# VectorE's operands in a fused attention and feed-forward kernel: q's scale through PSUM, the first keys transposed as fp32

## The chip, the core and the metric

The kernel runs on one NeuronCore of a Trainium2 chip. A core has a matrix engine (TensorE, PE in the profile), a vector engine (VectorE, DVE), an activation engine (ScalarE, ACT), a general engine (GpSimd, POOL) and a synchronisation engine (SyncE, SP) that here issues DMAs. Each works through its own instructions in order; semaphores make one wait for another. On-chip data lie in SBUF, matmul results in PSUM, which has eight banks of 512 fp32 columns for each of 128 partitions. POOL works on data in SBUF alone in this kernel.

The metric is device time in microseconds, the median over several executions of the whole program.

## What is computed

```python
# q, k, v: [8, 8, 576, 64] (batch, head, token, dim); w_phi: [64, 128]
def phi(x):
    proj = np.einsum('bhsd,df->bhsf', x, w_phi)
    proj = proj - np.max(np.abs(proj), axis=-1, keepdims=True)
    return np.concatenate([np.exp(proj), np.exp(-proj)], axis=-1)
q_p, k_p = phi(q), phi(k)
kv  = np.einsum('bhsf,bhsd->bhfd', k_p, v)
z   = np.sum(k_p, axis=2)
num = np.einsum('bhsf,bhfd->bhsd', q_p, kv)
den = np.einsum('bhsf,bhf->bhs', q_p, z)[..., None] + 1e-06
x   = (num / den) -> [4608, 512]
gate = np.maximum(x @ w_gate, 0.0)          # [512, 1536]
out  = (gate * (x @ w_val)) @ w_out         # -> [4608, 512] fp32
```

Linear attention with a feature map, and behind it a gated feed-forward network (FFN). In the feature map each row is shifted by the maximum of its absolute projections. The shift of q cancels between numerator and denominator for exp(proj) and exp(-proj) only up to a factor exp(2 max) between the two halves, so the kernel takes unshifted exponentials and applies that factor later.

## The kernel before

**Tiling.** The 8 batches follow each other. Of each batch's 576 tokens the first 512 are handled as 4 chunks of 128 tokens for each of 8 heads, two heads at a time (u = 0 to 3); the last 64 tokens of all heads are gathered in tiles of their own (names with an m: km, vm, qm). Matmuls run in bf16 with fp32 sums. The FFN runs on groups of 512 tokens: group g is batch g's 512 tokens, a ninth group holds the remaining tokens of all batches. Group 0 is cut into two halves of 256 tokens, so that it can begin after two chunks.

**Steps of a batch.** The keys (kn) are turned so that dim lies on partitions (kT), by PE for batches 0 and 1 (turn_pe), by transposing DMAs on SP's queue afterwards. k_item multiplies two heads with w_phi (L537), takes the row maxima on VectorE (mk, L548) and the exponentials on ScalarE (kp, L511), computes exp(max) and its inverse (ek, L520 and L523) and scales v with them on POOL (vs, L563 and L570). k_rest does the same for the last tokens (kpm, mkm, vsm at L604 and L610); in batch 0 its scaling may go to POOL or VectorE. k_kv multiplies kp with vs (L631) and copies the result to SBUF (kv, L638). For q, q_cols forms the projections (L655), their maxima (mq, L665) and exponentials (qp). q_scale turns the maxima with an fp32 transpose (away, L682), takes a maximum into the SBUF tile xq (L688), spreads it to zq by a product with the constant tile one_a or one_b (L694), and turns it back by a matmul (L702); its exponential is cq. Batch 0 uses q_scale_rows instead (mr at L732, cr at L742). q_num multiplies qp with kv (L763), and VectorE adds the two halves with the scale: t (L771), u (L778), the inverse of the denominator r (L788). The quotient xu (L791) is a product with two SBUF inputs; it is made on POOL, and in batch 0 on POOL or VectorE. xu is transposed to xT, by PE in batch 0 (L804, L811), by DMA on SP later. The FFN takes x to val and gate (L833, L839, L842) and to the output (L864, L874, store L879).

**The start.** The space of w_out (wo_sb) is not needed early, so the first batch's k is loaded as fp32 into wo_sb (in pieces of heads 0-1, 2-3, 4-7 and the last tokens, on SP's queue) and cast to bf16 in kn and km by five casts at L918, on POOL, ScalarE or VectorE; then turned. w_phi's load goes out behind the first piece of k. Other loads: k, v, q of later batches and the weights, on the queues of SP and POOL. POOL issues its loads between its compute instructions, in order. PE fills waits of the first 24 us with matmuls on a tile of zeros (L353).

**Order.** A planner written into the kernel decides it when the program is built: op(...) records each step with the engines that it may run on, a duration for each, what it depends on, the buffers and PSUM banks that it takes, and a key for its priority. Plan.run then plays the steps through and writes each engine's instructions in that order. Changing a duration, an engine or a buffer of one step can change the order of everything after it. FFN steps have a late key and fill what attention leaves free. Loads and DMA transposes are kept apart: transposes wait until the loads issued before them are done, and the other way round.

Of the kernel before, what the change touches and what calls it, by code (L numbers as in the profile page):

```python
# [9 lines left out]
FP32 = mybir.dt.float32  # L10
# [239 lines left out]
def kernel(  # L250
# [11 lines left out]
    nc = tc.nc  # L262
# [23 lines left out]
    def ring(name, n, shape, dtype=BF16):  # L286
# [20 lines left out]
        "mkm": ring("mkm", 2, [P, NU], FP32),  # L307
        "ekm": ring("ekm", 2, [P, NU, 2], FP32),
        "mq": ring("mq", 2, [P, NQ, C * H], FP32),
        "xq": ring("xq", 1, [P, 32], FP32),  # L310
        "zq": ring("zq", 1, [P, NQ, 32], FP32),
        "cq": ring("cq", 2, [P, C * H], FP32),
        "mqm": ring("mqm", 1, [P, NQ, H], FP32),
# [46 lines left out]
    def bank():  # L360
        return Buf(R["ps"])
# [14 lines left out]
            rows_ = slice(D * hh, D * (hh + 1))  # L376
            nc.vector.tensor_copy(w2[rows_, hh, :], w32[rows_])

    o_w32 = op(SP, 0.53, load_w, key=(0, 0.5), kind="l", nbytes=2 * D * F * 4)
    o_w = op(DVE, 0.3, cast_w, [o_w32], key=(2, 0, -30.0))  # L380

    def clear_w():
# [89 lines left out]

    def turn_pe(src, dst, n, dst_buf, deps, key, src_buf):

        ps = bank()

        def mm():
            pt = ps.t.bitcast(BF16)  # L480
            s = src()
            for i in range(n):
                nc.tensor.matmul(
                    pt[:, P * i : P * (i + 1)], lhsT=s[:, P * i : P * (i + 1)], rhs=ident,
                    is_transpose=True,
                )

        def out_(eng):
            f = nc.scalar.copy if eng is nc.scalar else eng.tensor_copy
            f(dst(), ps.t.bitcast(BF16)[:, 0 : n * P])  # L490

        a = op(PE, 0.057 * n, mm, [*deps, o_ident], [src_buf, dst_buf], [ps], key, "a")
        return op((ACT, DVE), {ACT: act(P * n), DVE: 0.06 + 0.0675 * n}, out_, [a], [dst_buf],
                  [ps], key, "a")

    def turn_dma(src, dst, nbytes, dst_buf, deps, key, src_buf, pad=1.0):
        def go():
# [80 lines left out]
    def k_rest(b, kmT, turned, vm, o_v, key, dve_scale=False):  # L578
        kp, m, e, vs = buf("kpm"), buf("mkm"), buf("ekm"), buf("vsm")
        ps = bank()  # L580

        def rows():
            for i in range(2):
                nc.tensor.matmul(
                    ps.t[:, 2 * F * i : 2 * F * (i + 1)],
                    lhsT=kmT.t[:, i, :],
                    rhs=w2.rearrange("p a f -> p (a f)"),
                )

        def amax():  # L590
            nc.vector.tensor_reduce(
                m.t, ps.t.rearrange("p (c f) -> p c f", f=F),
                axis=AX.X, op=ALU.max, apply_absolute_value=True,
            )

        a = op(PE, 0.22, rows, [turned, o_w, o_wz], [kmT, kp, m, e, vs], [ps], key, "a")
        r = op(DVE, 0.6, amax, [a], [m], [ps], key, "a")
        ex = exps(ps, lambda s: kp.t[:, s], kp, [a], key, F)
        o_e = e_of(m, e, [r], key)
        sc = []  # L600
        for x in range(2):
            def scale(eng, x=x):
                rows_ = slice(SM * x, SM * (x + 1))
                eng.tensor_tensor(  # L604
                    vs.t[rows_, :, x, :, 0:D],
                    vm.t[rows_][:, :, None, :].to_broadcast([SM, NU, 2, D]),
                    e.t[rows_][:, :, :, None].to_broadcast([SM, NU, 2, D]),
                    op=ALU.mult,
                )
                eng.tensor_copy(vs.t[rows_, :, x, :, D], e.t[rows_])  # L610

            engs = (POOL, DVE) if dve_scale else (POOL,)
            sc.append(op(engs, {POOL: 1.12, DVE: 1.9}, scale, [o_e, o_v, o_clear], [vm, e, vs],
                         key=key, kind="a"))
        return kp, vs, ex, sc
# [56 lines left out]
            exd.append(exps(ps, dst, qp, [a], key, P))  # L672
        return reds, exd

    def q_scale(mq, xq, zq, cq, n, deps, key):

        ps = bank()
        cols = NQ * n
        one, pick = (one_a, pick_a) if n > H else (one_b, pick_b)

        def away():
            nc.tensor.matmul(  # L682
                ps.t[0:cols, 0:P], lhsT=mq.t.rearrange("p j c -> p (j c)"), rhs=ident32,
                is_transpose=True,
            )

        def amax():
            nc.vector.tensor_reduce(  # L688
                xq.t[0:cols], ps.t[0:cols, 0:P].rearrange("p (g t) -> p t g", g=NQ),
                axis=AX.X, op=ALU.max,  # L690
            )

        def spread():
            nc.vector.tensor_tensor(  # L694
                zq.t[0:cols],
                xq.t[0:cols][:, None, :].to_broadcast([cols, NQ, 32]),
                one[0:cols][:, :, None].to_broadcast([cols, NQ, 32]),
                op=ALU.mult,
            )

        def back():
            nc.tensor.matmul(  # L702
                ps.t[:, P : P + n], lhsT=zq.t[0:cols].rearrange("p j t -> p (j t)"),
                rhs=pick[0:cols],
            )

        def ex():
            nc.scalar.activation(cq.t, ps.t[:, P : P + n], AF.Exp, scale=2.0)

        a = op(PE, 0.13, away, [*deps, o_consts], [mq, xq, zq, cq], [ps], key, "a")  # L710
        r = op(DVE, 0.2, amax, [a], [mq, xq], [ps], key, "a")
        z = op(DVE, 0.2, spread, [r, o_consts], [xq, zq], key=key, kind="a")
# [35 lines left out]
    def q_num(qp, exd, kv_of, cq, o_c, ccol, batches, dst, dst_buf, key, pe_turn=False):  # L748
# [44 lines left out]
            )  # L793

        o_r = op(DVE, 0.11, rec, us, [u, r], key=key, kind="a")
        o_x = op((POOL, DVE) if pe_turn else POOL, {POOL: 0.99, DVE: 0.61} if pe_turn else 0.99, div, [o_r], [u, r, xu], key=key, kind="a")
        flat = lambda: xu.t.rearrange("p h d -> p (h d)")
        if not pe_turn:
            return turn_dma(flat, dst, P * DM * 2, dst_buf, [o_x], key, xu)
# [95 lines left out]
    xTs, kv_of, mix_x = {}, {}, []  # L895
    ins = {}
    for b in range(B):
        ins[b] = {n: buf(n) for n in ("kn", "qn", "vn", "km", "vm")}
        if b % 2 == 1:
            ins[b]["qm"] = buf("qm")  # L900
    got = {}
# [5 lines left out]
    CAST = (POOL, ACT, DVE)  # L907

    def heads_of(b, name, src, en, lo, hi, key, deps=(), pad=0.0):
        o = load_main(b, name, src, en, slice(lo, hi), key, ins[b][name], deps, pad)  # L910
# [1 line left out]
            got[name, b, h] = o  # L912
        return o

    def cast(src, dst, n, deps, key, dst_buf, engs):
        def go(eng):
            f = nc.scalar.copy if eng is nc.scalar else eng.tensor_copy
            f(dst(), src)  # L918

        return op(engs, {e: {POOL: 0.06 + n * 0.00105, DVE: 0.06 + n * 0.00055, ACT: act(n)}[e]  # L920
                         for e in engs},
                  go, deps, [dst_buf], key=key, kind="a")


    k_heads = ((0, 2), (2, 4), (4, 8))
    o_km = load_rest_by_head(0, k, SP, (0, 1.5), None, (), 0.0, km32)
    got["km", 0] = cast(km32, lambda: ins[0]["km"].t, NU * D, [o_km], (2, 0, 0, 5), ins[0]["km"],
                        CAST)
    for i, (lo, hi) in enumerate(k_heads):
        o = load_main(0, "kn", k, SP, slice(lo, hi), (0, i), None, (), 0.0, kn32)  # L930
        last_k = o
        for u in range(lo // 2, hi // 2):
# [49 lines left out]
    for b in range(B):  # L982
        first = b == 0
        if b > 1:
            later_loads(b)
        kn, qn, vn, km, vm = (ins[b][n] for n in ("kn", "qn", "vn", "km", "vm"))
        ak = (2, b)
        b0 = len(plan.ops)
        kT, qT, kmT = buf("kT"), buf("qT"), buf("kmT")
        kflat = lambda kn=kn: kn.t.rearrange("p h c d -> p (h c d)")  # L990
        qflat = lambda qn=qn: qn.t.rearrange("p h c d -> p (h c d)")
        kmf = lambda km=km: km.t.rearrange("p j d -> p (j d)")
        turned_k, tq = {}, []
        if b < TURNS:
            for u in range(NU):
# [5 lines left out]
                turned_k[2 * u] = turned_k[2 * u + 1] = o  # L1001
            o_kmT = turn_pe(kmf, lambda kmT=kmT: kmT.t.rearrange("p a b -> p (a b)"), 2, kmT,
                            [got["km", b]], (*ak, 0, 5), km)
            for x in range(2):
# [78 lines left out]
        else:  # L1083
            mq, cq = buf("mq"), buf("cq")
            chunks, reds = [], []
            for cp in range(C // 2):
                qps, rd, exd = q_two(cp, mq, (*ak, 1, cp))
                reds += rd
                chunks += [(qps[x], exd[x]) for x in range(2)]
            o_c = q_scale(mq, buf("xq"), buf("zq"), cq, C * H, reds, (*ak, 1, 9))  # L1090
# [9 lines left out]
        if b % 2 == 1:  # L1100
# [14 lines left out]
            o_cm = q_scale(mqm, buf("xq"), buf("zq"), cqm, H, reds, (*ak, 3))  # L1115
# [71 lines left out]
```

## Time and profile before

| | us |
|---|---|
| median of 5 runs | 410.76 |
| lowest, highest | 409.74, 412.99 |
| the profiled execution | 412.12 |
| its span, first to last instruction | 410.4 |

| engine | busy us | share of the span |
|---|---|---|
| PE (matmuls) | 384.6 | 94% |
| DVE | 290.1 | 71% |
| ACT | 224.7 | 55% |
| POOL | 166.1 | 40% |

The profile is that of one execution. The profile's page gives, for each group of instructions, the line of the kernel, the engine, the operation, output and inputs, its number, busy time and the mean duration of one, and then how long the engine sat idle before it and what ended that. A range of a line is given as minimum/median/maximum in nanoseconds. The timeline lists instructions by start, with durations in microseconds. The granted clock is the share of full speed that TensorE was given; it is 1.0 or 0.5 over pieces of about 3.4 us in this profile. Busy PE time isn't PE at its peak, since a matmul's end is modelled.

### The profile page before, as it was taken

What the parts mean: (1) busy time and instruction counts of PE and PEld (TensorE: products, weight loads), DVE (VectorE), ACT (ScalarE), POOL (GpSimd) and SP (SyncE); (2) the same over time, 40 slices, a digit from 0 to 9 for tenths busy, and PEclk for the clock granted to TensorE, in tenths of its full rate; (3) what the DMA queues carried; (4) which work ended last, traced back from release to release, by engine and by line L of the source; (5) the groups of instructions that cost most, each with busy time, mean ns of one, the idle gap of its engine ahead of it and who ended that gap; (6) DMA issues with size and microseconds to landing.
All of it is one profiled execution on the core that took longest, in us unless ns stands there. A gap on an engine that the chain in (4) does not pass through costs nothing.

```text
span 410.4 us, 8667 instructions
## 1 busy us (share of the span) xinstructions
PE 384.6 (94%) x3268; PEld 209.8 (51%) x3268; DVE 290.1 (71%) x685; ACT 224.7 (55%) x486; POOL 166.1 (40%) x196
## 2 busy tenths in 40 slices
PE   7696999989999979999789999999999999999995
PEld 6574688543645535554245545445554444444442
DVE  6899877598797769889949999758974333433432
ACT  4599984079878448849814696559411311311310
POOL 2975844138598319634934492617131000000000
PEclk9799899989999989999969999999999999999998
DMA  6999299686956944985953397440022002002004
GB/s 216 180 204 202 51 181 198 141 136 103 169 109 135 228 98 76 155 157 138 260 110 100 91 120 136 130 143 0 15 66 90 2 26 77 2 26 78 0 3 99
DMA packets 86187, 45.65 MB, mean 111 GB/s; under 512 B 57666, under 2 KB 78786, under 8 KB 86146
## 3 DMA queue, kind: packets, MB, share of 16 engines
q0 software_dynamic: 29312, 20.65, 31.1%
q1 hardware_dynamic: 56834, 24.46, 25.2%
q8 instruction: 25, 0.41, 0.4%
q14 instruction: 16, 0.13, 0.1%
HBM read 37.81 MB, written 9.44 MB: 115 GB/s over the span
## 4 chain that ended last, share of the span: by engine, by line
PE 73%; DVE 12%; ACT 5%; issue 4%; POOL 3%; DMA 2%; SPq 0%; DVEq 0%; POOLq 0%; ACTq 0%
PE ps L833 38%; PE ps L864 22%; PE ps L631 4%; PE ps L763 4%; DVE mk L548 2%; DVE u L778 2%; DVE t L771 2%; PE ps L655 2%; ACT qp L511 2%; ACT kp L511 2%; DVE zq L694 2%; POOL vs L563 1%; PE ps L537 1%; DVE kn L918 1%; DMA wo_sb<-in_k_dram 1%
## 5 line engine op out<-in xcount | busy, mean ns | idle before, releaser
L839 ACT CAST val<-ps 128x512 bf16<-128x512 f32 (+1 forms) x120 | 68.9, 574 | 109.3 <-PE ps L833 104.6
L842 DVE SCALAR_TENSOR_TENSOR h<-ps,val 128x512 bf16<-128x512 f32 (+1 forms) x120 | 75.3, 630 | 56.6 <-PE ps L833 52.1
L833 PE MATMUL ps<-xT,wv_sb 128*128 128x512 bf16 (+1 forms) x432 | 102.8, 363 | 2.0 <-DVE xT L811 0.8
L833 PE MATMUL ps<-xT,wg_sb 128*128 128x512 bf16 (+1 forms) x432 | 104.3, 367 | 0.1
L864 PE MATMUL ps<-wo_sb,h 128*128 128x512 bf16 x432 | 99.7, 379 | 0.1
L511 ACT ACTIVATE qp<-ps 128x512 bf16<-128x512 f32 x144 | 78.1, 678 | 12.8 <-PE ps L655 7.5
L511 ACT ACTIVATE kp<-ps 128x512 bf16<-128x512 f32 x128 | 70.7, 644 | 23.2 <-PE ps L537 22.2
L791 POOL TENSOR_TENSOR xu<-u,r 128x512 bf16<-128x512 f32 x35 | 36.3, 1044 | 86.2 <-DVE r L788 50.5
L563 POOL TENSOR_TENSOR vs<-vn,ek 128x1024 bf16<-128x1024 f32 x32 | 61.2, 1911 | 23.7 <-PE ps L833 17.7
L833 PEld LDWEIGHTS <-wg_sb 128*128 128x128 bf16 x480 | 45.8, 101 | 44.2 <-issue 5.6
L833 PEld LDWEIGHTS <-wv_sb 128*128 128x128 bf16 x480 | 45.1, 100 | 44.6 <-issue 5.9
L864 PEld LDWEIGHTS <-h 128*128 128x128 bf16 x432 | 40.3, 98 | 45.6 <-issue 2.4
L874 DVE COPY ob<-ps 128x512 f32<-128x512 f32 x29 | 19.9, 686 | 34.4 <-PE ps L864 34.4
L548 DVE TENSOR_REDUCE mk<-ps 128x4 f32<-128x512 f32 x64 | 40.7, 671 | 3.0 <-PE ps L537 1.8
L778 DVE TENSOR_TENSOR u<-ps,t 128x195 f32<-128x195 f32 (+3 forms) x120 | 36.4, 328 | 3.0 <-POOL xu L791 1.7
L665 DVE TRANSPOSE_TENSOR_REDUCE mq<-ps 128x16 f32<-128x512 f32 x56 | 36.4, 688 | 1.6 <-PE ps L655 1.5
L763 PEld LDWEIGHTS <-qp 128*128 128x128 bf16 x640 | 28.3, 98 | 12.1 <-issue 1.5
L763 PE MATMUL ps<-kv,qp 128*128 128x65 bf16 x640 | 31.6, 193 | 0.3 <-DVE u L778 0.2
L771 DVE TENSOR_TENSOR t<-ps,cq 128x195 f32<-128x195 f32 (+1 forms) x84 | 24.6, 327 | 3.1 <-PE ps L763 2.8
L631 PEld LDWEIGHTS <-kp 128*128 128x128 bf16 x512 | 21.7, 99 | 3.2 <-issue 0.6
L631 PE MATMUL ps<-vs,kp 128*128 128x65 bf16 x512 | 22.4, 195 | 0.0
L631 PE MATMUL ps<-vsm,kpm 128*128 128x65 bf16 x128 | 20.5, 194 | 0.0
(90 smaller groups left out, 329.6 us busy)
## 6 DMA issues: line engine op xcount, KB each, us to landing
out_dram<-ob SPq DMA_DIRECT2D x32, 256.0 KB, 2.3
vn<-in_v_dram POOLq DMA_DIRECT2D x6, 1024.0 KB, 9.1
qn<-in_q_dram POOLq DMA_DIRECT2D x8, 512.0 KB, 7.0
kn<-in_k_dram POOLq DMA_DIRECT2D x7, 512.0 KB, 6.4
wo_sb<-in_moe_w_out_dram POOLq DMA_DIRECT2D x1, 1536.0 KB, 12.4
vn<-in_v_dram SPq DMA_DIRECT2D x2, 512.0 KB, 6.0
vn<-in_v_dram SPq DMA_DIRECT2D x1, 1024.0 KB, 7.7
wv_sb<-in_moe_w_val_dram POOLq DMA_DIRECT2D x1, 1024.0 KB, 10.7
```

Source lines behind the costliest of these rows:

```text
L511: nc.scalar.activation(dst(s), ps.t.rearrange("p (c f) -> p c f", f=f), AF.Exp, scale=sign)
L548: nc.vector.tensor_reduce(m.t.rearrange("p (i x) -> p x i", x=2)[:, x], ps.t.rearrange("p (c f) -> p c f", f=F), axis=AX.X, op=ALU.max, ap ...
L563: eng.tensor_tensor(vs.t[:, :, :, 0:D], vn.t[:, 2 * u : 2 * u + 2].rearrange("p h c d -> p (h c) d")[:, :, None, :] .to_broadcast([P, 2 * ...
L631: nc.tensor.matmul(acc[:, hh, s, :], lhsT=lhsT, rhs=rhs, start=(n == 0), stop=(n == 19))
L665: nc.vector.tensor_reduce(mdst(x), ps.t.rearrange("p (h j t) -> p h j t", j=NQ, t=32), axis=AX.X, op=ALU.max, apply_absolute_value=True, a ...
L763: nc.tensor.matmul(ps.t[:, E * (2 * i + s) : E * (2 * i + s + 1)], lhsT=qp.t[:, s, h, :], rhs=kv_of[b][h // 2][0].t[:, h % 2, s, :],)
L778: nc.vector.tensor_tensor(u.t[rows, lo : lo + n], ab[:, :, 0], t.t[rows, 0:n], op=ALU.add)
L791: eng.tensor_tensor(xu.t, u.t[:, :, 0:D], r.t.to_broadcast([P, H, D]), op=ALU.mult)
L833: nc.tensor.matmul(ps.t[:, 0:n], lhsT=w[:, dc, P * fi : P * fi + P], rhs=xt()[:, dc, lo:hi], start=(dc == 0), stop=(dc == NDC - 1),)
L839: nc.scalar.copy(val.t[:, 0:n], pv.t[:, 0:n])
L842: nc.vector.scalar_tensor_tensor(h.t[:, fi, lo:hi], pg.t[:, 0:n], 0.0, val.t[:, 0:n], op0=ALU.max, op1=ALU.mult,)
L864: nc.tensor.matmul(ps.t, lhsT=h.t[:, fi, P * t : P * t + P], rhs=wo_sb[:, fi, :], start=(fi == 0), stop=(fi == NFC - 1),)
```

## The change

Four things are edited:

- q_scale's maxima are written to columns 256 to 287 of the PSUM bank that the step already holds, and spread reads them there. The tile xq is gone.
- The two steps that could run on VectorE with two SBUF inputs, div (xu) in batch 0 and the scaling of k_rest in batch 0, are given to POOL alone.
- Batch 0's k isn't cast any more. turn_pe transposes the fp32 data with an fp32 identity into an fp32 bank, and the copy out of PSUM makes it bf16. Batch 0 takes no kn and km buffers, and the load of w_out, which overwrites the space, waits for the transposes instead of the casts.
- w_phi is loaded first on SP's queue.

```diff
-        "xq": ring("xq", 1, [P, 32], FP32),
...
-    o_w32 = op(SP, 0.53, load_w, key=(0, 0.5), kind="l", nbytes=2 * D * F * 4)
+    o_w32 = op(SP, 0.53, load_w, key=(0, -1), kind="l", nbytes=2 * D * F * 4)
...
-    def turn_pe(src, dst, n, dst_buf, deps, key, src_buf):
+    def turn_pe(src, dst, n, dst_buf, deps, key, src_buf=None):
         ps = bank()
+        wide = src_buf is None
+        pt = lambda: ps.t if wide else ps.t.bitcast(BF16)
         def mm():
-            pt = ps.t.bitcast(BF16)
             s = src()
             for i in range(n):
                 nc.tensor.matmul(
-                    pt[:, P * i : P * (i + 1)], lhsT=s[:, P * i : P * (i + 1)], rhs=ident,
-                    is_transpose=True,
+                    pt()[:, P * i : P * (i + 1)], lhsT=s[:, P * i : P * (i + 1)],
+                    rhs=ident32 if wide else ident, is_transpose=True,
                 )
         def out_(eng):
             f = nc.scalar.copy if eng is nc.scalar else eng.tensor_copy
-            f(dst(), ps.t.bitcast(BF16)[:, 0 : n * P])
+            f(dst(), pt()[:, 0 : n * P])
...
-            engs = (POOL, DVE) if dve_scale else (POOL,)
+            engs = (POOL,)
...
         def amax():
             nc.vector.tensor_reduce(
-                xq.t[0:cols], ps.t[0:cols, 0:P].rearrange("p (g t) -> p t g", g=NQ),
+                ps.t[0:cols, 2 * P : 2 * P + 32],
+                ps.t[0:cols, 0:P].rearrange("p (g t) -> p t g", g=NQ),
                 axis=AX.X, op=ALU.max,
             )
         def spread():
             nc.vector.tensor_tensor(
                 zq.t[0:cols],
-                xq.t[0:cols][:, None, :].to_broadcast([cols, NQ, 32]),
+                ps.t[0:cols, None, 2 * P : 2 * P + 32].to_broadcast([cols, NQ, 32]),
                 one[0:cols][:, :, None].to_broadcast([cols, NQ, 32]),
                 op=ALU.mult,
             )
...
-        o_x = op((POOL, DVE) if pe_turn else POOL, {POOL: 0.99, DVE: 0.61} if pe_turn else 0.99, div, [o_r], [u, r, xu], key=key, kind="a")
+        o_x = op((POOL,), 0.99, div, [o_r], [u, r, xu], key=key, kind="a")
...
-        ins[b] = {n: buf(n) for n in ("kn", "qn", "vn", "km", "vm")}
+        ins[b] = {n: buf(n) for n in ("kn", "qn", "vn", "km", "vm") if b or n[0] != "k"}
...
-    got["km", 0] = cast(km32, lambda: ins[0]["km"].t, NU * D, [o_km], (2, 0, 0, 5), ins[0]["km"],
-                        CAST)
+    got["km", 0] = o_km
...
-            c_ = cast(
-                kn32[:, 2 * u : 2 * u + 2], lambda u=u: ins[0]["kn"].t[:, 2 * u : 2 * u + 2], 2 * W,
-                [o], (2, 0, 0, u), ins[0]["kn"], CAST,
-            )
-            got["kn", 0, 2 * u] = got["kn", 0, 2 * u + 1] = c_
+        for h in range(lo, hi):
+            got["kn", 0, h] = o
...
-    o_wo = load_out((*low, 6), [o_wg[1], got["km", 0], *(got["kn", 0, 2 * u] for u in range(NU))])
+    o_wo = load_out((*low, 6), [o_wg[1]])
...
+            if wide:
+                o_wo.deps += [*turned_k.values(), o_kmT]
```

The order that the planner gives the changed program differs in these places that the next section speaks of. At the start VectorE, not ScalarE, copies the turned q out of PSUM; the kv matmuls of batch 0 all stand behind q's projections; POOL's four vs and two vsm of batch 0 stand together, before POOL's load of batch 1's k. On SP's queue three of the six later batches have their two kT transposes apart, with stores or xT transposes between them.

More of the change, by code (lines that the diff above doesn't have):

```diff
@@ L489, in out_ @@
             f = nc.scalar.copy if eng is nc.scalar else eng.tensor_copy
-            f(dst(), ps.t.bitcast(BF16)[:, 0 : n * P])
-        a = op(PE, 0.057 * n, mm, [*deps, o_ident], [src_buf, dst_buf], [ps], key, "a")
-        return op((ACT, DVE), {ACT: act(P * n), DVE: 0.06 + 0.0675 * n}, out_, [a], [dst_buf],
-                  [ps], key, "a")
+            f(dst(), pt()[:, 0 : n * P])
+        a = op(PE, (0.11 if wide else 0.057) * n, mm, [*deps, o_widen if wide else o_ident],
+               [dst_buf] if wide else [src_buf, dst_buf], [ps], key, "a")
+        return op((ACT, DVE), {ACT: act(P * n), DVE: dve(P * n) if wide else 0.06 + 0.0675 * n},
+                  out_, [a], [dst_buf], [ps], key, "a")
     def turn_dma(src, dst, nbytes, dst_buf, deps, key, src_buf, pad=1.0):
@@ L673, in q_cols, with q_scale @@
         return reds, exd
-    def q_scale(mq, xq, zq, cq, n, deps, key):
+    def q_scale(mq, zq, cq, n, deps, key):
         ps = bank()
@@ L708, in ex @@
             nc.scalar.activation(cq.t, ps.t[:, P : P + n], AF.Exp, scale=2.0)
-        a = op(PE, 0.13, away, [*deps, o_consts], [mq, xq, zq, cq], [ps], key, "a")
-        r = op(DVE, 0.2, amax, [a], [mq, xq], [ps], key, "a")
-        z = op(DVE, 0.2, spread, [r, o_consts], [xq, zq], key=key, kind="a")
+        a = op(PE, 0.13, away, [*deps, o_consts], [mq, zq, cq], [ps], key, "a")
+        r = op(DVE, 0.2, amax, [a], [mq], [ps], key, "a")
+        z = op(DVE, 0.2, spread, [r, o_consts], [zq], [ps], key, "a")
         b_ = op(PE, 0.13, back, [z], [zq], [ps], key, "a")
@@ L906 @@
     W = C * D
-    CAST = (POOL, ACT, DVE)
     def heads_of(b, name, src, en, lo, hi, key, deps=(), pad=0.0):
@@ L913, in heads_of @@
         return o
[L915 to L922, printed above, removed]
     k_heads = ((0, 2), (2, 4), (4, 8))
     o_km = load_rest_by_head(0, k, SP, (0, 1.5), None, (), 0.0, km32)
-    got["km", 0] = cast(km32, lambda: ins[0]["km"].t, NU * D, [o_km], (2, 0, 0, 5), ins[0]["km"],
-                        CAST)
+    got["km", 0] = o_km
     for i, (lo, hi) in enumerate(k_heads):
@@ L931 @@
         last_k = o
-        for u in range(lo // 2, hi // 2):
-            c_ = cast(
-                kn32[:, 2 * u : 2 * u + 2], lambda u=u: ins[0]["kn"].t[:, 2 * u : 2 * u + 2], 2 * W,
-                [o], (2, 0, 0, u), ins[0]["kn"], CAST,
-            )
-            got["kn", 0, 2 * u] = got["kn", 0, 2 * u + 1] = c_
+        for h in range(lo, hi):
+            got["kn", 0, h] = o
     heads_of(0, "vn", v, SP, 0, 4, (0, 4))
@@ L985 @@
             later_loads(b)
-        kn, qn, vn, km, vm = (ins[b][n] for n in ("kn", "qn", "vn", "km", "vm"))
+        kn, qn, vn, km, vm = (ins[b].get(n) for n in ("kn", "qn", "vn", "km", "vm"))
         ak = (2, b)
@@ L989 @@
         kT, qT, kmT = buf("kT"), buf("qT"), buf("kmT")
-        kflat = lambda kn=kn: kn.t.rearrange("p h c d -> p (h c d)")
+        wide = b == 0
+        if wide:
+            kn = km = None
+            kflat = lambda: kn32.rearrange("p h c d -> p (h c d)")
+            kmf = lambda: km32.rearrange("p j d -> p (j d)")
+        else:
+            kflat = lambda kn=kn: kn.t.rearrange("p h c d -> p (h c d)")
+            kmf = lambda km=km: km.t.rearrange("p j d -> p (j d)")
         qflat = lambda qn=qn: qn.t.rearrange("p h c d -> p (h c d)")
-        kmf = lambda km=km: km.t.rearrange("p j d -> p (j d)")
         turned_k, tq = {}, []
@@ L1003 @@
                             [got["km", b]], (*ak, 0, 5), km)
+            if wide:
+                o_wo.deps += [*turned_k.values(), o_kmT]
             for x in range(2):
@@ L1089 @@
                 chunks += [(qps[x], exd[x]) for x in range(2)]
-            o_c = q_scale(mq, buf("xq"), buf("zq"), cq, C * H, reds, (*ak, 1, 9))
+            o_c = q_scale(mq, buf("zq"), cq, C * H, reds, (*ak, 1, 9))
             for c, (qp, exd) in enumerate(chunks):
@@ L1114 @@
             exd = ex[0] + ex[1]
-            o_cm = q_scale(mqm, buf("xq"), buf("zq"), cqm, H, reds, (*ak, 3))
+            o_cm = q_scale(mqm, buf("zq"), cqm, H, reds, (*ak, 3))
             dummy = Buf(Ring("mix", [xT_mix]))
```

## Prediction

> **What bounds the kernel now.** First the table of busy time, then the waits of PE, then the duration ranges of single lines, then the timeline around the longest ones. The table:
>
> ```profile
> PE 384.6 (94%) x3268; PEld 209.8 (51%) x3268; DVE 290.1 (71%) x685; ACT 224.7 (55%) x486; POOL 166.1 (40%) x196
> ```
>
> TensorE is the bound. From 312.5 us on the chain of waits holds FFN matmuls alone, back to back (96 in 20.7 us, 216 ns each). All FFN and attention matmuls must run somewhere, so time falls only where PE stops losing some. The waits of PE (total, times, longest) name where it does:
>
> ```profile
> PE ps L702 <- DVE zq L694: 5.6, 2, 5.0
> PE ps L483 <- DVE kn L918: 5.0, 2, 3.5
> PE ps L537 <- DMA kT<-kn: 2.3, 2, 2.1
> ```
>
> The two largest are the two things the change edits. Their lines (min/median/max ns), beside a line whose inputs are one in PSUM and one in SBUF:
>
> ```profile
> L694 DVE TENSOR_TENSOR zq<-xq,one_a x7: 291/292/6341, 53.5 to 270.4; 128x128 f32<-128x128 f32 x7
> L918 DVE CAST kn<-wo_sb x3: 428/473/4416, 6.6 to 15.5; 128x512 bf16<-128x512 f32 x3
> L778 DVE TENSOR_TENSOR u<-ps,t x120: 252/349/367, 28.9 to 308.9; 128x195 f32<-128x195 f32 x64, 128x130 f32<-128x130 f32 x32, 64x195 f32<-64x195 f32 x16, 64x130 f32<-64x130 f32 x8
> ```
>
> One zq of seven took 6.34 us, one cast of three 4.42; of 120 u, spread over the whole attention, none passed 0.37. The timeline shows what ran beside the long zq (start, duration):
>
> ```profile
> 199.99 1.92 POOL L563 TENSOR_TENSOR vs<-vn,ek 128x1024 bf16<-128x1024 f32 x1
> ...
> 205.97 1.03 POOL L604 TENSOR_TENSOR vsm<-vm,ekm 64x512 bf16<-64x512 f32 x1
> 206.96 0.27 POOL L610 CAST vsm<-ekm 64x8 bf16<-64x8 f32 x1
> ```
> ```profile
> 200.81 6.34 DVE L694 TENSOR_TENSOR zq<-xq,one_a 128x128 f32<-128x128 f32 x1
> 207.08 0.68 DVE L842 SCALAR_TENSOR_TENSOR h<-ps,val 128x512 bf16<-128x512 f32 x1
> ```
>
> POOL ran without a gap to 207.23; zq ended at 207.15. The next h, and with it the FFN's banks, waited for it. After it PE was slow as well (busy of PE, PEld, DVE, ACT, POOL; then granted clock):
>
> ```profile
> 206.70:213.60 6.90, 6.39 (x30) 3.08 (x31) 2.27 (x4) 0.78 (x2) 1.74 (x4) 0.51 0.54 105
> ```
>
> **Part 1: zq reads PSUM.** The amax writes its 32 columns into the bank (11 runs, 286 ns before; PSUM as target has no row, a few tens of ns either way, under 0.3 us in all), and spread has one input in SBUF, like u and t. Expected 0.29 us always. Gone: 6.34 - 0.29 = 6.05 us of VectorE. For PE this is at least those 6.05 us (h, and so the banks, come that much sooner), at most its 5.03 us idle plus 3.4 (about 6.8 us at half clock): 8.4. I take 7.0, nearer the lower end, because PE between 200 and 220 us wouldn't have run at its peak either.
>
> Two rules are weighed here. The Trainium skill, "SBUF — State Buffer", section "SBUF: two separate sides", has a VectorE operation with two SBUF inputs wait for one GpSimd instruction that came first. The longest near it is 1.94 us, so by the rule zq would take at most 2.2 and part 1 bring 1.9. The row says 6.34, across four POOL operations: the row decides. And "TensorE: Matmul & The Clock Gate", Part 1, lets the clock return after at least one busy window of about 3.4 us, so 1.7 lost at the least. The row has it at half for two such windows, 3.4 lost. With the rule's least the upper end would be 6.7.
>
> **Part 2: the first k.** Casts gone: 3 on DVE (5.2 us), 2 on ACT (1.0). The long one stood here (idle before it in brackets):
>
> ```profile
> 11.17 4.81 DVE L918 CAST kn<-wo_sb 128x512 bf16<-128x512 f32 x2
> ...
> 17.99 2.07 ACT L511 ACTIVATE kp<-ps 128x512 bf16<-128x512 f32 x4 [4.49 <-PE ps L537]
> ...
> 23.84 2.14 ACT L511 ACTIVATE qp<-ps 128x512 bf16<-128x512 f32 x4
> ```
> ```profile
> 28.39 0.62 DVE L771 TENSOR_TENSOR t<-ps,cr 128x195 f32<-128x195 f32 x2
> ```
>
> ACT idled 4.49 us, and is busy from 20 to 50 us. Added: 18 transposes in fp32. No row has a series of them; singly L682 has 282 ns, four bf16 ones took 0.40 us. Bounds 0 to 3 us more; I take twice the bf16, about 2 us. PE fills this stretch with 119 dummy matmuls (L353), which hide it; without them it would be 2 us. kT leaves PSUM as fp32: about 0.61 on ACT (L839's row) instead of 0.72, 0.69 on DVE (L874's) instead of 0.42, four copies. Moving w ahead of k on SP costs the first k its issue, 0.72 us; but the first exps waited for DVE behind the second k, landing at 6.6, and the issue of the rest stays within 0.1 us. Nothing.
>
> The new order, worked forward from the rows. ACT begins its exps at 7.96 as before: 18 x 0.53, five small ones of 0.2, two kT copies of 0.6 give 19.7; q landed at 15.2 and its copy has moved to DVE, so qp starts there, **4.1 us sooner**. DVE turns to q at 15.7, mr runs 17.7 to 22.7 (8 x 0.62). What is late next is POOL: with the DVE option gone it does four vs of 2.0 and two vsm of 1.3 from 11.4, to 22.0, and the changed order has all kv matmuls behind q's. Four of 0.6 us, the last behind a bank that ACT frees at 25.2, put the first t near 26.6 instead of 28.39; the fourth r, without DVE's xu (0.98) but with one more kT copy, near 37.1 instead of 39.8. The FFN starts some 2.0 us sooner.
>
> On the queues: POOL issues k of batch 1 behind its scales, at 22.0 instead of 17.83. It needs 6.1 us to land, so 28.1; its transposes stood at 28.87. That cover is under 1 us; beyond it each us delays batch 1. The rest of the up weights goes out near 26.7 instead of 28.6. The load of w_out now waits for the transposes, long done at its 48.9. Batch 0 takes no kn and km buffers any more; that frees slots which no load waits for, since the later ones are held behind w_out's. Part 2: 2.0 us, from 0 (POOL and kv take all) to 3.5.
>
> **Part 3: POOL keeps div and vsm.** In the profile DVE did one of each (0.98 and 0.68). Moving them adds 1.04 and 1.04 to POOL, 40% busy; in the sum above. 0.
>
> **The sum.** 7.0 + 2.0 = 9.0 us. Against the profiled execution, 412.12 (span 410.4), that is 403.1; it lies 1.4 above the median, from which I forecast 410.76 - 9.0 = 401.8, said as **402**. The ends of both parts (8.4 + 3.5 and 6.05 + 0) give 398.9 and 404.7; with 1 us for the spread of the runs its own range is 398 to 406.
>
> **Rivals.** The planner moves everything after the start, and each has its place there.
>
> *Half is given back (20%).* The attention is paced elsewhere by ACT and POOL, or kv eats the start: part 1's lower end less half, 3, plus 0.8: **407**. For it: PE from 90 to 300 us has waits too short to be listed. Against: FFN matmuls from finished batches are always there to fill.
>
> *The stall only moves (12%).* The change doesn't do what it says: spread still waits behind POOL since it writes SBUF and reads one_a there. Then part 1 brings nothing and kv leaves some 0.8 of part 2: **410**. Against: 120 u and 120 t of just this kind, max 367.
>
> *Slower (13%): kT behind xT on SP.* That queue is in order. Before, both kT transposes of each of six batches stand together; in the changed program three pairs are split, by a store, by an xT, and by xTs and a store, which wait for POOL's xu or an FFN's end. The price is on the third line of waits: PE idle up to 2.1 us for kT, then a window at half clock (148.7 to 152.1), 1.7: 3.8 each, 11.4 for three. **413**. It decides from 3 us each on. For it: SP waited 33.2 us for POOL's xu. Against: most kT are needed much later than issued.
>
> **Chances.** A change under 0.5%, 2 us, can't be told from none here. Faster: 55 + 20 = 75%; same 12%; slower 13%. The range runs from 397.5, both parts at their upper ends (398.9) and the spread of the runs below it, to 410.5, which holds the stalled case and leaves the slow one out.
>
> **What would show it.** zq at most 0.35 us in all 11; no PE wait for zq above 0.5; no half clock behind it; ACT without the 4.5 us gap and the first qp near 20; the first t near 26.6. Wrong: one zq above 1 us; first t after 28.4; PE waits on kT above 4 us in sum.

## The result and the profile after

The changed kernel takes **407.11 us** (median of 44 runs, 404.76 to 412.64) against 410.56 us for the kernel before (79 runs, 405.67 to 414.38): a ratio of 0.993, with a 95% interval of 0.9916 to 0.9945. That is 3.4 us less, faster by 0.7% by the ratio, and well short of the 8.8 us that were forecast. Medians here are over all runs; ratios and their intervals leave out the runs that took over 1.5% longer than the fastest of the same kernel, so the two can differ by some tenths of a per cent. The profiled execution of the changed kernel took 406.73 us, its span 405.0 us.

The table of busy time of the changed kernel (engine, us, share of the span, instructions):

```profile
PE 381.1 (94%) x3264; PEld 207.3 (51%) x3264; DVE 279.4 (69%) x686; ACT 219.5 (54%) x477; POOL 166.4 (41%) x199
```

VectorE has lost 10.7 us of work, ScalarE 5.2, TensorE 3.5. The waits of PE (who it waited for: total, times, longest) tell what came of it:

```profile
PE ps L541 <- DMA kT<-kn: 3.2, 1, 3.2
PE ps L486 <- DMA kn<-in_k_dram: 2.9, 1, 2.9
PE ps L588 <- DMA kmT<-km: 2.5, 2, 2.0
PE ps L809 <- POOL xu L796: 1.8, 2, 1.4
```

The two waits at the head of the old list, 5.6 us for zq and 5.0 us for the cast, are gone. Three waits for transfers stand at the head now: the first k of batch 1 at 30.5 us, a transposed k at 84.8 us, a transposed km at 263.2 us. The zq instructions themselves are as forecast (min/median/max ns, first and last start):

```profile
L699 DVE TENSOR_TENSOR zq<-ps,one_a x7: 280/292/292, 52.7 to 285.9; 128x128 f32<-128x128 f32 x7
L699 DVE TENSOR_TENSOR zq<-ps,one_b x4: 260/268/278, 61.1 to 295.8; 32x128 f32<-32x128 f32 x4
```

None of the 11 is longer than 0.292 us, where one took 6.34. So both stalls are gone, and 3.4 us came of it. The question is where the rest went.

### The profile page after: what moved, and what is told of

The parts are those of the page before. It is cut to its first block, busy times and chain, and to the rows that moved or that the text cites. A ratio compares the mean times of both kernels' runs of the same rounds, so it can differ in the third digit from the quotient of the medians.

```text
span 405.0 us, 8662 instructions
## 1 busy us (share of the span) xinstructions
PE 381.1 (94%) x3264; PEld 207.3 (51%) x3264; DVE 279.4 (69%) x686; ACT 219.5 (54%) x477; POOL 166.4 (41%) x199
## 4 chain that ended last, share of the span: by engine, by line
PE 78%; DMA 8%; ACT 4%; DVE 3%; POOL 2%; issue 2%; SPq 2%; DVEq 0%; ACTq 0%
PE ps L838 44%; PE ps L869 19%; PE ps L635 4%; PE ps L768 4%; PE ps L659 2%; PE ps L541 2%; DMA vm<-in_v_dram 2%; DMA qT<-qn 2%; DMA kn<-in_k_dram 2%; ACT kp L515 2%; POOL vs L567 1%; DMA kT<-kn 1%; DMA wo_sb<-in_k_dram 1%; SPq L502 1%; DVE u L783 1%
## 5 line engine op out<-in xcount | busy, mean ns | idle before, releaser
L844 ACT CAST val<-ps 128x512 bf16<-128x512 f32 (+1 forms) x120 | 70.1, 589 | 100.3 <-PE ps L838 92.1
L838 PE MATMUL ps<-xT,wg_sb 128*128 128x512 bf16 (+1 forms) x432 | 101.1, 359 | 0.4 <-ACT val L844 0.3
L515 ACT ACTIVATE qp<-ps 128x512 bf16<-128x512 f32 x144 | 79.9, 730 | 3.7 <-PE ps L659 3.5
L796 POOL TENSOR_TENSOR xu<-u,r 128x512 bf16<-128x512 f32 x36 | 37.4, 1044 | 105.8 <-DVE r L793 68.2
L879 DVE COPY ob<-ps 128x512 f32<-128x512 f32 x30 | 20.7, 690 | 35.6 <-PE ps L869 33.9
L783 DVE TENSOR_TENSOR u<-ps,t 128x195 f32<-128x195 f32 (+3 forms) x120 | 35.5, 327 | 0.5
L768 PE MATMUL ps<-kv,qp 128*128 128x65 bf16 x640 | 30.0, 195 | 0.2 <-DVE kv L642 0.2
L776 DVE TENSOR_TENSOR t<-ps,cq 128x195 f32<-128x195 f32 (+1 forms) x84 | 23.6, 327 | 6.0 <-PE ps L768 5.7
```

What stands on the lines that cost most here:

```text
L515: nc.scalar.activation(dst(s), ps.t.rearrange("p (c f) -> p c f", f=f), AF.Exp, scale=sign)
L768: nc.tensor.matmul(ps.t[:, E * (2 * i + s) : E * (2 * i + s + 1)], lhsT=qp.t[:, s, h, :], rhs=kv_of[b][h // 2][0].t[:, h % 2, s, :],)
L783: nc.vector.tensor_tensor(u.t[rows, lo : lo + n], ab[:, :, 0], t.t[rows, 0:n], op=ALU.add)
L796: eng.tensor_tensor(xu.t, u.t[:, :, 0:D], r.t.to_broadcast([P, H, D]), op=ALU.mult)
L838: nc.tensor.matmul(ps.t[:, 0:n], lhsT=w[:, dc, P * fi : P * fi + P], rhs=xt()[:, dc, lo:hi], start=(dc == 0), stop=(dc == NDC - 1),)
L844: nc.scalar.copy(val.t[:, 0:n], pv.t[:, 0:n])
```

## The experiments

Twelve programs, of which e4 and e11 are known ones run again. "Order held" means that every engine's instructions stand in the order of the kernel before, apart from those the edit itself removes or adds; the planner would otherwise move everything behind the edit. Times are medians in us, beside the kernel before on the same chip.

| kernel | what differs | time | before | ratio, 95% interval |
|---|---|---|---|---|
| e1 | before, maxima in PSUM, order held | 407.94 | 410.36 | 0.998, 0.9943 to 1.0018 |
| e2 | before, fp32 k, order held | 409.47 | 410.36 | 0.9983, 0.9946 to 1.0021 |
| e3 | both of these, order held | 407.20 | 410.36 | 0.994, 0.991 to 0.997 |
| e4 | before, unchanged (one run) | 410.56 | 410.36 | |
| e5 | e3, xu and vsm on POOL | 406.91 | 410.54 | 0.9924, 0.9895 to 0.9952 |
| e6 | after, maxima in SBUF again | 407.47 | 410.54 | 0.9918, 0.9883 to 0.9953 |
| e7 | after, v of batch 1 behind its k | 416.23 | 410.54 | 1.014, 1.0099 to 1.018 |
| e8 | after, batch 2's loads earlier | 407.52 | 410.54 | 0.9894, 0.9854 to 0.9935 |
| e9 | after, k of batch 1 earlier | 407.92 | 410.43 | 0.9938, 0.9899 to 0.9976 |
| e10 | e8 and e9 together | 405.25 | 410.43 | 0.9872, 0.9833 to 0.9911 |
| e11 | after, unchanged | 407.12 | 410.43 | 0.9919, 0.9891 to 0.9947 |
| e12 | e10, one kmT ahead of two xT on SP | 403.23 | 410.13 | 0.9825, 0.9782 to 0.9868 |

### e1 to e4: each part alone, in the old order

e1 has only these lines of the change, e2 only those of turn_pe and of the casts (which stay in the plan and issue nothing), e3 both:

```diff
-                xq.t[0:cols], ps.t[0:cols, 0:P].rearrange("p (g t) -> p t g", g=NQ),
+                ps.t[0:cols, 2 * P : 2 * P + 32],
+                ps.t[0:cols, 0:P].rearrange("p (g t) -> p t g", g=NQ),
...
-                xq.t[0:cols][:, None, :].to_broadcast([cols, NQ, 32]),
+                ps.t[0:cols, None, 2 * P : 2 * P + 32].to_broadcast([cols, NQ, 32]),
```
```diff
-            f = nc.scalar.copy if eng is nc.scalar else eng.tensor_copy
-            f(dst(), src)
+            return None
...
-                    4, kT, [got["kn", b, 2 * u]], (*ak, 0, u), kn,
+                    4, kT, [got["kn", b, 2 * u]], (*ak, 0, u), kn, wide=first,
```

> The kernel before with q's maxima kept in PSUM and nothing else: every engine's order is that of before, so only the two operations of q's scale differ. Theory A (the 6 us stall is in every execution and PE pays for all of it, 7.0 us by the prediction): zq at most 0.3 us, no PE wait for it, about 403.5 us, ratio 0.983. Theory B (the stall is only in some executions, or its time is lost again behind it): 407 to 410 us, ratio 0.992 to 1.0. Zq stays long: the operation waits behind POOL for another reason than its second SBUF input.

> The kernel before with the first k transposed as fp32 and the five casts gone, the order of all other instructions held, zq as before. Theory A (part 2 is worth about 2 us for itself): ACT's gap of 4.5 us before the third kp is gone, ratio 0.993 to 0.997. Theory B (what the start wins is lost at the next wait, the landing of a load or kT): the first exps come earlier but the time is within 0.3% of before.

> Both edits at once, with the order of before held on every engine (the planner is still told of the casts). If the gains are real and the new order gave part of them back, this is faster than the changed kernel: Theory A 401 to 404 us, ratio 0.978 to 0.985. Theory B (the stall or the start is worth little by itself): 406 to 408 us, like the changed kernel, ratio near 0.993.

> The kernel before, unchanged, profiled once more. Theory A: one zq near 200 us again takes about 6 us and the second cast about 4.4. Theory B: in this execution the zq of the same place is short or the long one is another, since it depends on whether POOL's run of scales falls together with it.

The medians say that part 1 brings about 2.4 us, part 2 about 0.9, and both together 3.2. By the ratios it is 0.8, 0.7 and 2.5. The intervals of e1 and e2 alone still touch 1; that of e3 doesn't. So a gain of both together is shown, but not how it divides between them. What e1 does exclude is the forecast for part 1: its interval ends at 2.3 us, where at least 6.05 were expected. The stall itself is no accident of one execution: the longest zq is 6.34 us in the first profile, 6.79 in e4 and 6.62 in e2, each ending within 0.1 us of the first gap in POOL's work, and 0.29 in e1 and e3.

Why only 2.4? Since the order is held, the programs can be laid side by side at the same instructions. The table gives the time from one start to the next in us; the seventh zq is the one that stalled, and the ninth had a stall of its own of 2.2 us. Each column is one execution.

| stretch | before | e4 | e1 | e3 | e5 |
|---|---|---|---|---|---|
| start to the seventh zq | 200.8 | 199.7 | 201.7 | 199.3 | 200.2 |
| seventh zq to the eighth | 20.9 | 19.7 | 15.6 | 18.4 | 17.9 |
| eighth zq to the end of VectorE's work | 184.8 | 185.5 | 184.9 | 184.6 | 185.1 |

All of the gain lies in the second row: 20.3 on the mean with the stall, 17.3 without, so 3.0 us. (e2 keeps the stall and has 21.0 there, in a profiled execution of 414.74 us.) The stall of 2.2 us at the ninth zq was worth nothing that shows; PE waited 0.6 us for it. And the earlier start of e3 and e5 shows in the first row by no more than the rows of before differ among themselves.

PE in the kernel before, from the end of the stall to the first kv matmul (start, duration, idle time before it in brackets):

```profile
207.21 0.64 PE L702 MATMUL ps<-pick_a,zq 128*128 128x32 f32 x2 [5.03 <-DVE zq L694]
...
212.76 0.43 PE L631 MATMUL ps<-vs,kp 128*128 128x65 bf16 x4
```

The kv matmuls wait for nothing there: POOL's last vsm ended at 208.5, while PE stood and then did three groups of FFN matmuls. What took the stall's place is in e1's timeline. POOL first (start, duration):

```profile
204.71 1.90 POOL L563 TENSOR_TENSOR vs<-vn,ek 128x1024 bf16<-128x1024 f32 x1
206.56 0.24 POOL L570 CAST vs<-ek 128x16 bf16<-128x16 f32 x1
206.71 1.03 POOL L604 TENSOR_TENSOR vsm<-vm,ekm 64x512 bf16<-64x512 f32 x1
207.69 0.21 POOL L610 CAST vsm<-ekm 64x8 bf16<-64x8 f32 x1
207.98 1.04 POOL L604 TENSOR_TENSOR vsm<-vm,ekm 64x512 bf16<-64x512 f32 x1
208.96 0.22 POOL L610 CAST vsm<-ekm 64x8 bf16<-64x8 f32 x1
```

Then PE in the same kernel, with its idle time in brackets:

```profile
207.95 0.19 PE L631 MATMUL ps<-vsm,kpm 128*128 128x65 bf16 x1 [2.00 <-POOL vsm L610]
...
209.24 0.19 PE L631 MATMUL ps<-vsm,kpm 128*128 128x65 bf16 x1 [0.82 <-POOL vsm L610]
```

The run of POOL work that had held zq is the run that makes vs and vsm, and the kv matmuls, which stand in PE's queue a few FFN matmuls behind the place where zq is needed, can't start before it ends. Free of zq, PE does those FFN matmuls early and then waits for the same POOL run: 2.8 us in e1, 3.1 in e3, 3.7 in e5. Of PE's 5.0 us of idle time for zq, 2.2 is left as gain in e1. The half clock behind the stall isn't gained for good either, since the new idle time can bring it as well. The same 20 us of before, of e1 and of e3 (busy of PE, PEld, DVE, ACT, POOL; granted clock, DMA share, GB/s):

```profile
200.00:220.00 20.00, 14.97 (x153) 8.34 (x152) 13.71 (x20) 6.29 (x15) 10.03 (x13) 0.83 0.64 140
```
```profile
200.00:220.00 20.00, 17.18 (x192) 10.04 (x190) 12.77 (x36) 9.53 (x22) 10.74 (x14) 1.00 0.88 165
```
```profile
200.00:220.00 20.00, 16.91 (x180) 10.89 (x178) 10.75 (x30) 7.13 (x17) 10.59 (x14) 0.83 0.75 150
```

PE's busy time rises by 2.2 and 1.9 us of the 5.0 that it had stood idle. In e1 the clock is whole; in e3 it is at 0.83, as in before, at half from 205.6 to 212.4, where no zq stalls. This goes with the spread in the table: 15.6 us in e1, 17.9 and 18.4 in e5 and e3.

At the start, part 2 let the wait move. With the cast gone, VectorE's next operation with two SBUF inputs stood there instead (e3, by tile; min/median/max ns):

```profile
L605 DVE TENSOR_TENSOR vsm<-vm,ekm x1: 3209/3209/3209, 12.5 to 12.5; 64x512 bf16<-64x512 f32 x1
```

It takes 0.68 us in the profile of before. The change as a whole gives that instruction to POOL; e5 shows what that is worth.

### e5: the whole change in the old order

e3, and the two kinds of steps given to POOL where they are emitted (all but the place of w_phi's load and the planner's new order):

```diff
+        if o.fn.__name__ in ("scale", "div"):
+            e = POOL
```

> All edits of the change but the order of the start's weight loads, in the engine order of the kernel before, with vsm and xu of the first batch on POOL. Theory O (the planner's new order gave back what the edits brought): without that order the late loads of batch 2 and the PE waits of the changed kernel at 84.8 and 261 us are gone, so 402 to 404.5. Rival N (the two stalls were worth only about 3 us together, since the next wait stands right behind each): 406 to 408, the same as with both edits and the old order, though DVE's vsm of 3.2 us at 12.6 is gone.

406.91 us, 0.3 from e3 and 0.2 from the changed kernel. The rival held: the new order neither gains nor loses on balance, and VectorE's 3.2 us at the start were worth nothing that can be measured. In e5 PE waits 6.1 us for the loads of q instead. Part 3 at nothing was right.

### e6: part 1 taken out of the new order

```diff
-                ps.t[0:cols, 2 * P : 2 * P + 32],
-                ps.t[0:cols, 0:P].rearrange("p (g t) -> p t g", g=NQ),
+                xq[0:cols], ps.t[0:cols, 0:P].rearrange("p (g t) -> p t g", g=NQ),
```

> The changed kernel and its order, only the maxima back in an SBUF tile, so that the spread has two SBUF inputs again. Theory (a spread with two SBUF inputs waits until a run of POOL instructions ends): one or two zq above 2 us, where a zq stands beside a run of POOL work in the new order, and a PE wait for zq; 2 to 4 us slower than the changed kernel, about 410. Rival (the new order has moved POOL's runs away from every zq): all zq below 0.5 us and 407, so that the move to PSUM brings nothing in this order.

The rival held, nearly to the letter: the time is that of the changed kernel, and with two SBUF inputs the zq of the new order are (min/median/max ns)

```profile
L699 DVE TENSOR_TENSOR zq<-xq,one_a x7: 282/293/293, 53.6 to 286.3; 128x128 f32<-128x128 f32 x7
L699 DVE TENSOR_TENSOR zq<-xq,one_b x4: 255/268/1116, 62.0 to 296.2; 32x128 f32<-32x128 f32 x4
```

In the new order POOL's run of scales ends at 204.9 us and the zq of that batch starts at 211.0, so there is nothing left to wait for, beyond 1.1 us once. In the changed kernel the stall would have gone by the reordering alone, and the move to PSUM adds nothing that these runs can show. That e3 and the changed kernel gain the same is therefore not one sum found twice: in the new order part 1 has nothing to remove.

### e7 and e9: what holds the start

e7 lets v of batch 1 wait for its k to land; e9 has POOL issue k (and km) of batch 1 ahead of its two vsm of batch 0.

```diff
-    heads_of(1, "vn", v, SP, 0, H, (0, 15), [o_wg[0]]).gate = o_wg[0]
+    o_vn1 = heads_of(1, "vn", v, SP, 0, H, (0, 15), [o_wg[0]])
+    o_vn1.gate = o_kn1
```
```diff
+    k1 = [o_kn1, got["km", 1]]
+    vsm0 = [x for x in order if x[1] == POOL and x[0].fn.__name__ == "scale"][4][0]
+    order = moved(order, lambda o, e: o in k1, lambda o, e: o is vsm0)
```

> The changed kernel with v of batch 1 held until k of batch 1 has landed. Theory (k of batch 1, issued at 23.3, takes 7.2 us because v's 0.5 MB, issued at 20.8, shares the DMA engines): k lands at 27 to 28, the PE wait of 2.9 us for it falls below 1, and the window at half clock behind it goes: 403.5 to 405.5. Rival (k's landing is set by its own issue and its descriptors): it still lands after 30, the wait stays above 2 us, and v of batch 1 comes later as well: 407 to 409.

> The changed kernel with the loads of k of batch 1 issued by POOL at about 20.9 us, ahead of its two vsm of batch 0, instead of at 23.3 behind them; nothing else moves. Theory T (the start is bound by its transfers up to about 44 us, and the changed kernel leaves the DMA engines half idle from 20.8 to 23.3): k lands at 26 to 28 instead of 30.5, the PE wait of 2.9 us for it is gone, the last weights land near 42.5 instead of 44.4, the first zq stands near 51 instead of 52.7; 1.5 to 2 us faster than the changed kernel. Rival P (POOL's scales pace the start): the two vsm and with them all kv come 2.2 us later, the first t stands at 28.5 or later, and nothing or a loss up to 2 us comes of it.

Issue and landing of the loads of batch 1 and of the rest of the up weights, by the trace (us), and the first zq, which ends the start:

| | k | v | q | w_val | w_gate | first zq |
|---|---|---|---|---|---|---|
| before | 17.8 to 23.9 | 20.3 to 28.0 | 26.3 to 32.4 | to 39.4 | to 44.3 | 53.45 |
| after | 23.3 to 30.5 | 20.8 to 26.4 | 25.5 to 33.6 | to 39.4 | to 44.4 | 52.75 |
| e9 | 20.7 to 30.5 | 20.7 to 26.1 | 25.4 to 33.4 | to 39.4 | to 44.4 | 53.31 |
| e7 | 22.6 to 28.6 | 28.6 to 47.0 | 24.8 to 33.3 | to 42.5 | to 48.4 | 51.72 |

e9 refutes my theory in the way that tells most: k was issued 2.6 us sooner and landed at the same 30.5. What moved in e9 from 20 to 25 us shows why (queue: packets, MB, share of the DMA engines; q1 is SP's, with v, and q0 POOL's, with k):

```profile
q1 hardware_dynamic: 907, 0.93, 62.8%
q0 software_dynamic: 7, 0.01, 0.7%
```

v and k were issued at 20.70 and 20.74 us. The 7 packets of q0 all lie before 20.4 us and belong to an earlier load, so k moved nothing until almost all of v's 1.0 MB had. In before, after and e9 the set of loads ends at 34.1 to 34.5 (the last piece of q), 39.4 and 44.4, whichever comes first among them. Who is served first changes; the end doesn't. The recorded rival came too: the two vsm, behind the loads now, end 2.1 us later and the first t stands at 29.50 us, 2.8 later, so e9 alone doesn't say which of the two kept its time from falling. In e7, k and batch 1 are indeed served first (k 1.9 us sooner, the first zq 1.0 us sooner), and v, with 1.0 MB and not the 0.5 of the expectation, pays: the kv of batch 1 then wait up to 5.2 us for vsm, and in the ten us behind it PE stands. The windows of e7, then of after:

```profile
50.00:60.00 10.00, 3.24 (x49) 2.94 (x48) 1.73 (x6) 3.27 (x8) 9.93 (x13) 0.82 0.24 30
```
```profile
50.00:60.00 10.00, 9.94 (x171) 8.89 (x170) 8.16 (x24) 8.09 (x21) 3.52 (x6) 1.00 1.00 148
```

That is 416.23 us, 9 us worse. I read this as a start that is held by its transfers more than by the work of its engines, so that an earlier start of batch 0 buys little; no run made the transfers themselves shorter, so this is argued. Nor were the DMA engines full throughout: from 20 to 22 us their share is 0.13 in after and in e9. How much reached batch 1 is in the timelines of after, TensorE first and then VectorE:

```profile
30.52 1.07 PE L486 MATMUL ps<-ident,kn 128*128 128x128 bf16 x16 [2.88 <-DMA kn<-in_k_dram]
```
```profile
26.70 0.62 DVE L776 TENSOR_TENSOR t<-ps,cr 128x195 f32<-128x195 f32 x2
```

The first t stands 1.69 us earlier than before; then PE waits 2.88 us for batch 1's k, and the first zq has 0.7 left. One thing stays open: from ScalarE's second exp of batch 1's k to the first zq it takes 20.0 us in the new order (19.45 to 20.25 in eight programs), but 17.8 to 18.5 in five of six programs of the old one. The new order needs more for the same work. About 1 us of it stands right at the beginning, where the next pair of heads follows 2.8 to 3.4 us behind that exp instead of 1.7 to 2.5; the rest I haven't separated.

### e8, e10, e11 and e12: what the new order loses

e8 has POOL issue q and v of batch 2 ahead of two xu; e10 adds e9's move; e12 adds the move of one transpose on SP's queue.

```diff
+    order = moved(order, lambda o: o.key[:2] == (3, 2) and o.bytes and POOL in o.eng)
```
```diff
+    kmT7 = [o for o, e in order if e == "SP" and (o.key or ())[:2] == (2, 7)][2]
+    order = moved(order, lambda o, e: o is kmT7,
+                  lambda o, e: e == "SP" and (o.key or ())[:2] == (2, 6)
+                  and o.gate is kmT7.gate)
```

> The changed kernel with the loads of batch 2 (q, v) issued by POOL ahead of two xu instead of behind them; no other engine's order differs. Theory (the new order's late loads cost the PE wait of 3.2 us for kT at 84.8 and the two windows at half clock behind it): that wait and the windows go, and 3 to 5 us with them: 402 to 404. Rival (the loads are not what kT waits for; SP's place behind a store is): the wait stays above 2 us and the time at 406 to 408.

> The changed kernel with both moves on POOL: k of batch 1 ahead of two vsm, and batch 2's loads ahead of two xu. If the two losses (the wait at 30 us, the one at 84.8) stand on their own, the gains add: 402 to 404. If the kernel is held by its transfers elsewhere, 406 to 408, as with each alone.

> The changed kernel once more on the same chip as the two before it, for a comparison without other chips: 407, and 405 to 406 without the disturbed runs.

> The kernel with both loads early, and on SP's queue the transpose of km of batch 7 issued ahead of the two xT of batch 6 instead of behind them; nothing else moves. This prices one place of the rival that had kT behind xT on SP. Theory: PE's wait of 2.2 us for kmT at 264.7 and the window at half clock behind it (1.7 us lost) go, xT comes 1.2 us later and PE has other work for it: 402 to 403.5. Rival: the xT that now comes later is waited for instead, or the window falls elsewhere: 404.5 to 406, as without it.

e8 is open. Its median can't be told from e6's on the same chip (407.52 and 407.47); its ratio is lower (0.9894 against 0.9918), and the intervals overlap. The loads went out at 54.2 instead of 65.4, but SP issued the kT transpose at 79.55 instead of 79.98: the loads were not what held it, and PE's wait only fell from 3.2 to 2.0 us. e10 is 1.9 us below e11 in the medians, though the intervals overlap; its waits for k and for kT are 1.6 and 1.8 us instead of 2.9 and 3.2. The two windows at half clock behind kT remain.

e12 is clear of the changed kernel. SP's queue is in order, and in e10 it had (start, duration):

```profile
259.74 2.50 SPq L502 DMA_TRANSPOSE xT<-xu  x2
262.35 1.19 SPq L502 DMA_TRANSPOSE kmT<-km  x1
```

PE in e10 and, in the second fence, in e12:

```profile
264.72 0.39 PE L588 MATMUL ps<-w,kmT 128*128 128x256 bf16 x2 [2.21 <-DMA kmT<-km]
```
```profile
259.87 0.38 PE L588 MATMUL ps<-w,kmT 128*128 128x256 bf16 x2
```

With kmT first, PE doesn't wait for it, and no wait for the later xT has come in its place, only 0.8 us for VectorE's ob. The median falls by 2.0 us, to **403.23 us**. That fits the wait of 2.2; six runs on each side leave the intervals of e10 and e12 overlapping, and the half clock that the expectation put behind the wait isn't in e10's profile. The six runs of e12 lie between 402.49 and 404.06, below every one of the changed kernel's. This is the version that beats both: 6.9 us below the kernel before, 3.9 below the changed one, by two places on POOL's queue and one on SP's.

## Why the prediction was wrong

Point by point, in the order of its steps.

- **zq at 0.29 us, in all 11.** Right: 0.26 to 0.29. The maxima's write into PSUM costs 285 ns on the mean of 11, against 278 into SBUF. Of the two readings of the long zq, the row was the right one: the Trainium skill ("SBUF — State Buffer", section "SBUF: two separate sides") has such an operation wait for one GpSimd instruction, and three profiled programs have it at 6.34 to 6.79 us, across four multiplications and the small casts between them, until POOL's first gap.
- **Part 1 brings TensorE 7.0 us, at least 6.05.** This is the step that failed. It measured 2.4 in the medians (0.8 by the ratio) and 3.0 in its stretch. I took it that h, and so the banks, coming sooner carries over to the end. But the kv matmuls stand a little way behind in PE's own queue and need POOL's vsm, which ends at 208.5 us in before and at 209.2 in e1, stall or none; free of zq, PE waits there 2.8 us in e1, 3.1 in e3 and 3.7 in e5. The rows of POOL stood in the prediction's own timeline up to 207.23; I read them for who held VectorE and didn't ask who else waited for them. The lower end wasn't a lower end.
- **Of it, 3.4 us for the clock.** Not reliable: in e1 the half clock is gone, in e3 and e5 it comes back behind the new wait. By the Trainium skill ("TensorE: Matmul & The Clock Gate", Part 1) the full clock returns after at least one busy window of about 3.4 us; e3 shows two windows at half clock, as before did, and e4, with the stall, one.
- **Part 2 brings 2.0 us.** Probably too much by about 1.1: 0.9 in e2, 0.7 between e1 and e3; e2's interval reaches to 2.2, so 2.0 isn't excluded. The hand-worked start was right as far as the first t (ScalarE's first qp at 20.03, worked out 19.7; t at 26.70, worked out 26.6). Its weak term was the landing of batch 1's k at 28.1. It was 30.5, half of the miss from POOL (it issued the load at 23.3, worked out 22.0), half from the transfer, which took 7.2 us instead of 6.1. "Beyond it each us delays batch 1" was true. What was missing was a look at the DMA engines: their share was at or above 1.0 over most of 8 to 40 us in the profile of before, and in the changed kernel v of batch 1 is on its way when k is issued. "Nothing" for w ahead of k has no run of its own: in the changed kernel the first exps begin at 8.97 us, worked out 7.96, and at 7.58 in e5, which leaves w where it was. The fourth r stood at 38.65, worked out 37.1.
- **Part 3 at nothing.** Right (e5).
- **Half is given back: 407.** This rival came in size. In the old order it came in place as well: POOL paces the attention right behind the stall (e1). In the changed kernel's own order part 1 has nothing to remove (e6), so that its number fits there is in part luck.
- **kT behind xT and stores on SP, 3.8 us at each of three places.** The mechanism is there, at one of the three places and at a kmT that the rival didn't name, at a lower price: PE waits 3.2 us at 84.8 for the first kT of a split pair, which left SP behind an xT and took 4.8 us to land (in e10 it waits 1.8 us for the second, behind a store), and 2.0 at 263.2 for a kmT behind two xT. The kmT that was priced alone, in e12, is worth about 2.0 us.

So in the old order the edits bring 2.5 to 3.2 us (e3), and the changed kernel ends in the same place by another way. Its new order costs about the 3.9 us that e12 gets back with three moves, each of which puts a load or a transpose earlier again, as it stood in the kernel before (there at 17.8, 54.6 and 250.5 us). It gains about as much in other places; the stall that goes without part 1 (e6) is one, and the others were not separated.

## What to carry to other kernels

When a stall goes, look at what the same cause feeds besides the stalled instruction: the run of POOL work that held VectorE here also made the operands of TensorE's next matmuls, so more than half of TensorE's idle time came back as another wait. A second stall, for which TensorE waited only 0.6 us, was worth nothing that shows. At the start, computing sooner brought little, and a load that was issued sooner still moved behind the one that was issued beside it. In a program whose order is planned, hold the old order and make one edit at a time; the last gain came from moving three places in in-order queues, not from faster instructions.

## What the hardware showed that was not expected

A load that was issued 2.6 us sooner (e9) took 9.8 us instead of 7.2 and landed at the same moment, although the DMA engines' share was only about 0.5 between 20 and 24 us in both. In that stretch only SP's queue moved data, and POOL's k began at 25 us; why the two queues didn't share the engines from the start is open. And an idle time of 2.9 us on TensorE was followed by one window at half clock (31.8 to 35.2 us in the changed kernel), one of 3.2 us, with 0.9 us more inside the next window, by two (86.4 to 93.2), and one of 2.0 us by one (263.9 to 267.3) or by none (e1, at 208 us). These traces don't settle which it will be.
